# Attention and two feed-forwards on one core: an order that charges for array forms, shared transposes, feed-forward blocks of 512 tokens

## The chip, the cores and the metric

The kernel runs on one core of a Trainium2 chip. The metric is the device time of one execution in microseconds. The kernel before took 1044.32 us, the median of three runs (1043.76 to 1046.07).

## The reference

Three layers follow each other, all in 32-bit floats.

```python
# attention: q, k, v [4, 8, 576, 64], s [4, 8, 576]
scores = q @ k.T / 8                                   # causal
cum = cumsum(maximum(s, 0)); bias = -(cum[i] - cum[j]) # at most 0
attn = softmax(scores + minimum(bias, 0)); x = attn @ v
# heads joined: x [2304, 512]
h = x @ w_in            # [2304, 2048]
x = (h * cos(h)) @ w_out
# x scaled by its root mean square and rms_g, then
y = (silu(xn @ w_gate) * (xn @ w_val)) @ w_out2   # inner width 1536
```

The weights come as float64 and are turned to float32 on the chip.

## The kernel before, in words

**The order.** The program first collects operations (`plan.op`), each with an engine or several that could do it, a cost in ns, the buffers it reads and writes, and a priority, which is a due time (`plan.now`). `Plan.order` then plays them through: the engine that is free first takes, of the operations that are ready, the one with the earliest due time, and its cost moves that engine's clock. The result is a fixed order of instructions on every engine; on the chip each engine works through its own list and waits at semaphores. Two users of one buffer (a slot of a ring, or overlapping bytes of an "arena") are kept in the order in which the program created them.

**Attention.** There are 16 pairs of heads (`Run`, one for each pair). The 576 queries are four tiles of 128 and a ragged one of 64; the ragged rows of the two heads of a pair lie together in one tile of 128 partitions (`"p"`). For each pair TensorE makes the scores: for the full tiles as two products of 64 contraction rows, one for each head, on the two halves of the array (L544; three such operations a pair), for the ragged tile as full products (L568). VectorE adds the bias and takes the minimum (L551, L571), ScalarE takes the exponential (L579), TensorE transposes the probabilities in pieces of 128x128 (`tr`, L594, 30 a pair), ScalarE and VectorE copy them out of PSUM to `Pa` and `Pb`, and TensorE multiplies with v, each head on 64 of the array's columns (L626; two operations a pair). So TensorE works in three forms: the full array, 64 rows by 128 columns (L544), and 128 rows by 64 columns (L626). `tr(e, i)` makes piece group `i` for head `e`. Groups 1 and 3 hold pieces of the ragged tile; both heads transpose the same five 128x128 pieces of it, and each copies its own 64 columns. Scores, transposes and v products of the first four pairs rotate over all eight PSUM banks, those of later pairs over banks 4 to 7 (`Run.bank`, L501). Attention's due times advance by `P_ATT` = 8000 ns a pair.

**First feed-forward.** Tokens go in nine blocks of 256. A step `k` of a block takes two of the 16 slices of 128 inner columns: `gemm1` (L723) makes h for both into one bank, 24 matmuls of 256 columns; ScalarE and VectorE make h * cos(h), split into two parts; `gemm2` (L729) adds 12 matmuls of 512 columns to the block's two accumulators (banks 0 and 1). h rotates over banks 2 and 3, from block 2 on over banks 2, 3 and 4 (`h_bank`). Steps are due every 8094 ns from 45000 ns on. Blocks 0 and 1 run beside attention, and beside block 0 the float64 weights are turned to float32 slices, two chunks of `w_in` and two of `w_out` for each step (`chunk`: L427, L428, L430, then a copy and a subtraction at L333 and L344). `w_out` chunks pass through four slots (`ws_r`), which `gemm2` frees. Blocks 2 to 8 run after attention, whose memory then holds `w_out`. At a block's end `rms_norm` copies its two accumulators out, finds the scale, and `rms_store` transposes (L810) and stores the rows.

**Second feed-forward.** Both products go by a scheme of seven block products in place of eight. `load_x2` loads 768 tokens at a time, forms four sums (`T1` to `T4`) and splits each of seven operands into two parts; `b` counts the three groups of tokens. L973 are the products with `w_gate` and `w_val`, in the order of operands 11, T2, T3, T1, 21, T4, 22; evacuations use slots `t` of 1536 bytes. The 20 slots (`t_spans`) lie in the arena `K`: ten at its upper half, ten at its lower 15 KB, where `load_x2` also stages its sums. L1114 are the products with `w_out2`.

Of the kernel before, what the change touches and what calls it, by code (L numbers as in the profile page):

```python
# [22 lines left out]
BLK1 = 256  # L23
NB1 = NT // BLK1
# [4 lines left out]
RMS_AT = 5  # L29
PAIRED = 0  # L30
# [7 lines left out]
SWITCH_PE = 90.0  # L38
# [11 lines left out]
class Op:  # L50
    __slots__ = ("alts", "prio", "table", "lat", "dma", "preds", "succs", "n", "ready", "eng", "cost", "start", "end", "fn", "seq", "rows")
# [31 lines left out]
class Arena:  # L83


    def __init__(self, plan, make, dtype):
        self.make, self.t, self.dtype, self.bufs = make, None, dtype, []
        plan.arenas.append(self)
# [41 lines left out]
class Plan:  # L130
# [27 lines left out]
    def order(self):  # L158
# [8 lines left out]
        for arena in self.arenas:  # L167
            held = {}
            for b in arena.bufs:
                mine = {o for o, _, _ in b.acc}  # L170
                cells = range(b.at // 256, -(-(b.at + 4 * b.n) // 256))
# [13 lines left out]
        table, dma_free, done, flying = None, 0.0, [], []  # L185
# [34 lines left out]
        while len(done) < len(self.ops):  # L220
# [9 lines left out]
            _, _, o = min((o.prio + (self.HOLD if o.table and o.table != table else 0.0), o.seq, o) for o in avail[e] if o.ready <= t)  # L230
            avail[e].remove(o)
            cost = o.cost
            if e == "PE":
                cost = clock(t, o) - t
# [43 lines left out]
def attention_moe_moe(ctx, tc, q2, k2, vp, s, w_in, w_out, w_gate, w_val, w_out2, rms_g, out):  # L278
# [38 lines left out]
    above = main.tile([128, 128], F32, name="above")  # L317
    pool.memset(above, 0.0)
    pool.affine_select(out=above, in_=above, pattern=[[-1, 128]], base=0, channel_multiplier=1, compare_op=ALU.is_ge, fill=BIG)
# [41 lines left out]
    def later(first, where, size):  # L361
        def make():
            stacks[first].close()
            pools[where] = spool(ctx, where, **ends[where][1])
            return pools[where].tile([128, size * KB // 4], F32R, name=where)
        return make

    A, G, K, R, Z = (Arena(plan, f, t) for f, t in (
        (lambda: wi_t, F32R), (lambda: wg_t, F32R), (lambda: f_t, F32), (later("att", "wr", 64), F32R), (later("x1", "x2", 16), F32R)))
# [12 lines left out]
    y_r = slots(K, 22 * KB, 2, (512,))  # L382
    xo_r = slots(K, 26 * KB, 1, (512,))
    rb_r = slots(K, 28 * KB, 1, (S,))
    st_r = ring("st", 2, [128, 8, 2], F32)
    x1_r = ring("xa", 4, [128, 2, 2, BLK1], F32R, "x1")
# [25 lines left out]
    xn_d = [dbuf(f"xn_d{j}", [128, 4, BLK1]) for j in range(NB1)]  # L412
# [34 lines left out]
    class Run:  # L447
# [52 lines left out]
        def bank(self):  # L500
            return psb("first", (0, 1, 2, 3, 4, 5, 6, 7)) if self.bp < 4 else psb("att", (4, 5, 6, 7))  # L501
# [15 lines left out]
    class Part:  # L517
# [12 lines left out]
        def score(self, ts):  # L530
# [15 lines left out]
            plan.op(on("PE", SWITCH_PE + sum(2.0 * w + 25 for _, w in at.values()), qk), [run.q, run.k], Sp)  # L546
# [11 lines left out]
        def score_p(self, g):  # L558
# [11 lines left out]
            plan.op(on("PE", 490 + SWITCH_PE / 2, qk), [run.q, run.k], [Sp], rows=0.9)  # L570
# [12 lines left out]
        def tr(self, e, i):  # L583
# [3 lines left out]
            srcs = {0: [((e, 0), 0, 128), ((e, 1), 0, 128), ((e, 1), 128, 128)], 1: [((e, 2), 128 * c, 128) for c in range(3)] + [("p", 512, 128)],  # L587
# [8 lines left out]
            plan.op(on("PE", 109 * len(srcs) + 40, go), [(E[0], E[1]) for E in Es], [tr], rows=0.5)  # L596
            cols = lambda n: tr()[:, :n].rearrange("p (c i) -> p c i", i=128)
            def out(o, src, n):
                copy(o, src, n, [tr], [P], psum=True)
# [3 lines left out]
            elif i == 1:  # L603
                out(lambda: P()[:, 0:3, 0:128], lambda: cols(384), 384)
                out(lambda: P()[:, 3, 0:64], lambda: tr()[:, 384 + 64 * e:448 + 64 * e], 64)
            elif i == 2:
                out(lambda: P()[:, :, 128:256], lambda: cols(512), 512)
            else:
                out(lambda: P()[:, :, 256:320], lambda: cols(512)[:, :, 64 * e:64 * e + 64], 256)

        def av(self):
# [16 lines left out]
            plan.op(on("PE", (710 if self.c == "a" else 2130) + SWITCH_PE, go), [vr, *P.values()], [X])  # L628
# [11 lines left out]
        def units(self):  # L640
            if self.c == "a":
# [4 lines left out]
                   [*(lambda e=e, i=i: self.tr(e, i) for i in (1, 3) for e in range(2)), self.av], False, True)  # L646
# [61 lines left out]
    def spin():  # L708
        for _ in range(WARM):
            pe.matmul(warm()[:, :128], ident, above, start=True, stop=True)  # L710
# [25 lines left out]
    def h_bank(j):  # L736
        return psb("h_late", (2, 3, 4)) if j >= RES else psb("h", (2, 3))

    def load_x1(j):
        xs = []  # L740
        for k0 in (0, 2):
            x = x1_r.new()
            raw = lambda x=x: x()[:, :, 1, :].bitcast(F32)
            lo, end = j * BLK1, (j + 1) * BLK1
            while lo < end:
                b, o = lo // S, lo // S * S
                hi = min(end, o + S)
                c0 = lo - j * BLK1
# [3 lines left out]
            copy(lambda x=x: x()[:, :, 0, :], raw, 512, [], [x])  # L752
            two(lambda x=x: x()[:, :, 1, :], raw, lambda x=x: x()[:, :, 0, :].bitcast(F32), 512, [], [x])
# [13 lines left out]
    for j in range(1, NB1):  # L767
        for f in range(F1):
            if j >= RES:
                continue  # L770
# [4 lines left out]
    def rms_norm(j, acc, late=0.0):  # L775
        st, ys = st_r.new(), []
        s0, ms, y, z = ((lambda i=i: st()[:, i, :]) for i in range(4))
        for t in range(2):
            v = y_r.new()
# [22 lines left out]
    def rms_store(j, ys):  # L802
        for k in (0, 2):

            tr, xo = h_bank(j + 1) if j < NB1 - 1 else bank.new(4), ys[0] if k else xo_r.new()

# [9 lines left out]
    acc = {}  # L816
    xs, ticks, todo = {}, {}, []

    def finish(k, h, u, g, less):
        j, m = divmod(k, 8)  # L820
        plan.now = tick_at(k) - LEAD_E
        plan.op(on("ACT", act_s(512) + 93, lambda: act.activation(u(), u(), AF.Sin, scale=-TWO_PI, bias=half_pi)), [], [u], table="sin", after=[less])  # L822
        two(u, h, u, 512, [h], [u], op=ALU.mult, psum=True)
        copy(lambda: g()[:, 0, :], u, 512, [u], [(g, 0)])
        two(lambda: g()[:, 1, :], u, lambda: g()[:, 0, :].bitcast(F32), 512, [u, (g, 0)], [(g, 1)])
        for i in range(2):
            plan.now = tick_at(k) + 1.6 * P_FF1
            f = 2 * m + i
            w = w2[j, f]
            plan.op(on("PE", 1400, lambda i=i, f=f, w=w, a=acc[j]: gemm2(  # L830
                [b() for b in a], [g()[:, a2, BLK1 * i:BLK1 * i + BLK1] for a2 in range(2)], w(), f == 0, f == F1 - 1)), [w, g], acc[j])

    for k in range(8 * NB1):
        j, m = divmod(k, 8)
        plan.now = tick_at(k) - 12000.0
        if m == 0:
            xs[j] = load_x1(j)
            acc[j] = [psb(f"acc{t}", (t,)) for t in range(2)]
        for f in (2 * m, 2 * m + 1):
            if j == RES:  # L840
                w2[j, f] = wr_r.new(f)
                load(lambda f=f: w2[RES, f]().bitcast(F32), wo_d[f], 1 << 19, [wo_d[f]], [w2[j, f]], after=[att_end, ticks[k - 4]])
            elif j > RES:
                w2[j, f] = w2[RES, f]
        h, u, g = h_bank(j), u_r.new(), g_r.new()
        for i in range(2):
            plan.now = tick_at(k)
            w = w1[2 * m + i]
            ticks[k] = plan.op(on("PE", 1440, lambda i=i, w=w, h=h, x=xs[j]: gemm1(h()[:, BLK1 * i:BLK1 * i + BLK1], w(), [b() for b in x], BLK1)), [w, *xs[j]], [h])
        plan.now = tick_at(k) - LEAD_E  # L850
        plan.op(on("ACT", act_p(512) + 93, lambda u=u, h=h: act.activation(u().bitcast(I32), h(), AF.Identity, bias=quarter)), [h], [u])  # L851
        less = two(u, lambda u=u: u().bitcast(I32), h, 512, [h], [u], psum=True)
        todo.append((k, h, u, g))
        if k >= PAIRED or k % 2:
            for args in todo:
                finish(*args, less)
            todo.clear()
        if k % 8 == 1 and j:
            plan.now = tick_at(k) - LEAD_E
            ys = rms_norm(j - 1, acc[j - 1])  # L860
        if k % 8 == RMS_AT and j:
            plan.now = tick_at(k) - LEAD_E
            rms_store(j - 1, ys)
    plan.now = tick_at(8 * NB1)
    rms_store(NB1 - 1, rms_norm(NB1 - 1, acc[NB1 - 1], RMS_LATE))


    T_FF2 = tick_at(8 * NB1 + 1)
# [39 lines left out]
    for n, (d, w, p) in enumerate(jobs):  # L908
        plan.now = tick_at(8 * NB1)
# [5 lines left out]

    X = {}
# [4 lines left out]
    def load_x2(b):  # L921
        for i in range(2):
# [5 lines left out]
            for q, to, o in ((0, raw("11"), x["11"]), (1, B12, B12), (2, raw("21"), x["21"]), (3, raw("22"), x["22"])):  # L928
                k, lo = i + 2 * (q // 2), b * 2 * HALF2 + (q % 2) * HALF2
                end, c0 = lo + HALF2, 0  # L930
                while lo < end:
                    j = lo // BLK1
                    hi = min(end, (j + 1) * BLK1)
                    op = load(lambda to=to, c0=c0, n=hi - lo: to()[:, c0:c0 + n], lambda j=j, k=k, lo=lo, hi=hi: xn_d[j]()[:, k, lo - j * BLK1:hi - j * BLK1],
                              512 * (hi - lo), [(xn_d[j], k // 2 * 2)], [(o, c0)])
                    if q != 1:
# [256 lines left out]
```

## Time and profile before

| | us |
|---|---|
| median of three runs | 1044.32 |
| lowest and highest | 1043.76, 1046.07 |
| the profiled execution | 1041.14 |
| its span, first to last instruction | 1039.40 |
| TensorE matmuls busy in it | 1006.5 |
| VectorE busy | 744.4 |
| ScalarE busy | 574.7 |
| GpSimd busy | 121.1 |
| mean granted clock of TensorE, of full speed | 0.992 |

The profiled execution is one run with the profiler on; its own time stands 1.74 us above its span, and 3.18 us under the median. "Busy" is the time in which at least one instruction of the engine was open. Matmuls overlap, so a busy TensorE still may have instructions of different spacing; the spacing is read from the starts of neighbouring rows.

### The profile page before, as it was taken

How to read it: one execution, taken by the hardware profiler on the slowest of the kernel's cores; microseconds unless marked ns; L12 is line 12 of the kernel's file. 1: busy time of each engine (PE TensorE's matmuls, PEld its weight loads, DVE VectorE, ACT ScalarE, POOL GpSimd, SP SyncE). 2: the span in 40 equal slices, each digit the busy share in tenths (PEclk: the TensorE clock that was granted, in tenths of full speed). 3: DMA queues.
4: the chain of work that ended last, by engine and by line, in shares of the span. 5: the costliest groups of instructions: out<-in, count | busy, mean ns of one | idle time of the engine just before them, and what ended most of it. 6: DMA issues, size and time to landing. Idle time of an engine off the chain costs nothing.

```text
span 1039.4 us, 19161 instructions
## 1 busy us (share of the span) xinstructions
PE 1006.5 (97%) x6594; PEld 897.6 (86%) x6594; DVE 744.4 (72%) x1693; ACT 574.7 (55%) x1236; POOL 121.1 (12%) x251
## 2 busy tenths in 40 slices
PE   7979998999999999999999999899999999999998
PEld 4646666767889999889989989899999999999998
DVE  7885888864436879878877795966566658986661
ACT  5877898897844656666654574311121124665540
POOL 3442453411000011100111000000000000000000
PEclk8999999999999999999999999999999999999999
DMA  8996798775485765657645545466374657997761
GB/s 276 317 334 191 235 309 299 230 247 171 128 296 233 243 239 187 235 196 254 237 169 172 164 125 189 135 204 203 114 233 120 216 177 233 304 318 223 221 196 42
DMA packets 146322, 223.86 MB, mean 215 GB/s; under 512 B 14656, under 2 KB 99792, under 8 KB 146224
## 3 DMA queue, kind: packets, MB, share of 16 engines
q1 hardware_dynamic: 146224, 222.64, 66.3%
q8 instruction: 52, 0.85, 0.3%
q14 instruction: 46, 0.38, 0.1%
HBM read 147.53 MB, written 75.06 MB: 214 GB/s over the span
## 4 chain that ended last, share of the span: by engine, by line
PE 61%; DVE 16%; DMA 12%; issue 5%; ACT 2%; POOL 1%; SPq 1%; POOLq 0%; DVEq 0%; ACTq 0%
PE bank L973 24%; PE bank L1114 13%; PE bank L723 8%; PE bank L729 7%; DVE wk L344 5%; DMA wk<-rn_d 3%; PE bank L626 3%; DVE wg L344 3%; PE bank L594 2%; DVE wk L428 2%; DMA wk<-in_w_out_dram 2%; PE bank L544 2%; DVE wk L430 2%; DMA wk<-in_w_gate_dram 1%; DMA wk<-in_w_val_dram 1%
## 5 line engine op out<-in xcount | busy, mean ns | idle before, releaser
L344 DVE TENSOR_TENSOR wk<-wk,bank 128x384 f32<-128x384 f32 (+2 forms) x315 | 173.0, 555 | 150.9 <-PE bank L973 72.7
L723 PE MATMUL bank<-xa,wi 128*128 128x256 f32 x1728 | 221.3, 283 | 0.1
L723 PEld LDWEIGHTS bank<-xa,wi 128*128 128x128 f32 x1728 | 215.5, 189 | 6.1 <-DVE wi L344 0.3
L729 PE MATMUL bank<-wr,wg 128*128 128x512 f32 x672 | 166.5, 396 | 0.8 <-ACT wg L333 0.7
L729 PEld LDWEIGHTS bank<-wr,wg 128*128 128x128 f32 x672 | 122.3, 188 | 26.8 <-ACT wg L333 1.4
L973 PE MATMUL bank<-wi,wg 128*128 128x384 f32 x504 | 116.8, 340 | 3.8 <-ACT wk L333 2.9
L973 PE MATMUL bank<-wr,wg 128*128 128x384 f32 x504 | 116.9, 340 | 0.0
L344 DVE TENSOR_TENSOR wg<-wk,wg 128x512 fp32r<-128x512 f32 (+1 forms) x148 | 91.4, 636 | 20.0 <-ACT wg L333 19.5
L333 ACT ACTIVATE wk<-bank 128x384 f32<-128x384 f32 (+2 forms) x79 | 40.0, 522 | 116.7 <-PE bank L973 83.6
L333 ACT ACTIVATE wg<-wk 128x512 fp32r<-128x512 f32 (+1 forms) x134 | 75.7, 576 | 49.0 <-DVE wk L344 38.2
L973 PEld LDWEIGHTS bank<-wi,wg 128*128 128x128 f32 x504 | 90.0, 189 | 5.8 <-ACT wk L333 3.4
L344 DVE TENSOR_TENSOR wk<-wk 128x384 f32<-128x384 f32 (+1 forms) x198 | 91.5, 503 | 0.7
L973 PEld LDWEIGHTS bank<-wr,wg 128*128 128x128 f32 x504 | 91.9, 189 | 0.0
L427 POOL TENSOR_SCALAR wk<-wk 128x512 f32<-128x512 f32 x68 | 50.8, 750 | 305.1 <-ACT wk L424 304.2
L579 ACT ACTIVATE e<-e,mn 128x128 f32<-128x128 f32 (+3 forms) x128 | 70.6, 554 | 16.4 <-DVE mn L551 15.8
L344 DVE TENSOR_TENSOR wk<-bank,wk 128x512 f32<-128x512 f32 (+1 forms) x90 | 59.3, 659 | 21.9 <-ACT wk L822 21.7
L822 ACT ACTIVATE wk<-wk,half_pi 128x512 f32<-128x512 f32 x72 | 52.2, 725 | 40.3 <-DVE wk L344 40.0
L333 ACT ACTIVATE wr<-wr 128x384 fp32r<-128x384 f32 x111 | 56.5, 523 | 31.5 <-DMA wr<-g_S 13.0
L1114 PE MATMUL bank<-wi,wr 128*128 128x256 f32 x585 | 73.7, 281 | 0.0
L851 ACT ACTIVATE wk<-bank,quarter 128x512 int32<-128x512 f32 x72 | 49.1, 682 | 41.7 <-PE bank L723 41.5
L1114 PEld LDWEIGHTS bank<-wi,wr 128*128 128x128 f32 x585 | 71.2, 188 | 0.0
L344 DVE TENSOR_TENSOR wr<-wr 128x384 fp32r<-128x384 f32 x111 | 58.0, 552 | 11.7 <-ACT wr L333 11.4
(114 smaller groups left out, 1493.6 us busy)
## 6 DMA issues: line engine op xcount, KB each, us to landing
wk<-in_w_out_dram SPq DMA_DIRECT2D x28, 512.0 KB, 6.5
g_S<-wk SPq DMA_DIRECT2D x72, 192.0 KB, 2.7
g<-wk SPq DMA_DIRECT2D x54, 192.0 KB, 2.4
wr<-g_S SPq DMA_DIRECT2D x54, 192.0 KB, 3.8
w_g<-wg SPq DMA_DIRECT2D x18, 512.0 KB, 4.9
w_v<-wg SPq DMA_DIRECT2D x18, 512.0 KB, 3.4
wr<-g SPq DMA_DIRECT2D x48, 192.0 KB, 3.5
wk<-in_w_in_dram SPq DMA_DIRECT2D x16, 512.0 KB, 5.5
```

The lines of the kernel that those rows point to most:

```text
L333: alts.append(("ACT", (act_p if psum else act_s)(n), lambda: act.activation(o(), i(), AF.Copy, scale=scale)))
L344: return plan.op(on("DVE", dve1(n), lambda: dve.tensor_tensor(out=o(), in0=a(), in1=b(), op=op)), r, w, **kw)
L427: plan.op(on("POOL", pool1(512), lambda: pool.tensor_scalar(out=top().bitcast(F32), in0=top().bitcast(F32), scalar1=0.0, scalar2=1.0, op0= ...
L428: plan.op(on("DVE", dve1(512), lambda: dve.scalar_tensor_tensor(out=top(), in0=low(), scalar=29, in1=top(), op0=ALU.logical_shift_right, o ...
L579: plan.op(on("ACT", act_s(w) + 187, lambda E=E, o=o, w=w, i=i, c=c: act.activation(E()[:, o:o + w], E()[:, o:o + w], AF.Exp, scale=-1.0, b ...
L626: pe.matmul(X()[64 * e:64 * e + 64, lo:hi], vr()[:kk, e, c, :], p[e], start=(c == 0), stop=(c == jobs[-1][0]))
L723: pe.matmul(h, w[:, a, 128 * k:128 * k + 128], x[k // 2][:, k % 2, c, :blk], start=(n == 0), stop=(n == 11))
L729: pe.matmul(acc[t], g[a][:, 128 * t:128 * t + 128], w[:, c, :], start=(first and (a, c) == (0, 0)), stop=(last and (a, c) == (1, 0)))
L822: plan.op(on("ACT", act_s(512) + 93, lambda: act.activation(u(), u(), AF.Sin, scale=-TWO_PI, bias=half_pi)), [], [u], table="sin", after=[ ...
L851: plan.op(on("ACT", act_p(512) + 93, lambda u=u, h=h: act.activation(u().bitcast(I32), h(), AF.Identity, bias=quarter)), [h], [u])
L973: pe.matmul(bank_()[:, :HALF2], G[i]()[:, u, o + 128 * k:o + 128 * k + 128], xs[k]()[:, c, :], start=(first and n == 0), stop=(n == 5), sk ...
L1114: pe.matmul(bk_()[:, col:col + 256], gs[p // 3]()[:, u, 128 * (p % 3):128 * (p % 3) + 128], w3[p][i]()[:, c, o:o + 256], start=(n == 0), s ...
```

## The change

It has these parts.

- **Order.** An operation on TensorE has a `mode` (0 full array, 1 the score products L544, 2 the v products L626). The order charges `SWITCH_PE` = 95 ns where the mode changes, and adds `KEEP_MODE` = 1000 ns to the due time of an operation that would change it. The modelled costs of these operations are changed to fit.
- **Ragged probabilities.** The five pieces of the ragged tile are transposed once for a pair; from the one result both heads' columns are copied.
- **Banks and pace of attention.** The first eight pairs use all eight banks (it was four pairs); `P_ATT` goes from 8000 to 6000.
- **Blocks of the first feed-forward.** Three of 256 tokens (the first two and the last) and three of 512. In a block of 512 a step takes one slice: 12 matmuls of 512 columns in `gemm1`, 12 of 512 columns in `gemm2`, into four accumulators (banks 0, 1, 5, 6). h rotates over banks 2, 3, 4 and 7. `rms_norm` runs twice at such a block's end, the two stores two steps apart.
- **Second feed-forward.** `load_x2` stages operand 11 in the slot of `T4` and makes the operands in the order in which the products take them, both halves of a group together. The `t` slots gain ten in a new arena `Y`, in memory of the x operands of the first feed-forward; these come first in the rotation.
- **Small ones.** The mask tile `above` is gone, and the warm-up multiplies the identity; the x ring holds 512 tokens a slot; the scratch memory for dynamic DMA is set to 1024.

```diff
+KEEP_MODE = 1000.0
-SWITCH_PE = 90.0
+SWITCH_PE = 95.0
-P_ATT, P_FF1, P_SET, P_OUT = 8000.0, 8093.98, 7350.0, 2145.0
+P_ATT, P_FF1, P_SET, P_OUT = 6000.0, 8093.98, 7350.0, 2145.0
+BLOCKS = ((0, 256), (256, 256), (512, 512), (1024, 512), (1536, 512), (2048, 256))
...
-            _, _, o = min((o.prio + (self.HOLD if o.table and o.table != table else 0.0), o.seq, o) for o in avail[e] if o.ready <= t)
+            _, _, o = min((o.prio + (self.HOLD if o.table and o.table != table else 0.0) + (KEEP_MODE if e == "PE" and o.mode != mode else 0.0), o.seq, o)
+                          for o in avail[e] if o.ready <= t)
...
-            return psb("first", (0, 1, 2, 3, 4, 5, 6, 7)) if self.bp < 4 else psb("att", (4, 5, 6, 7))
+            return psb("first", (0, 1, 2, 3, 4, 5, 6, 7)) if self.bp < 8 else psb("att", (4, 5, 6, 7))
...
-                out(lambda: P()[:, :, 256:320], lambda: cols(512)[:, :, 64 * e:64 * e + 64], 256)
+                for a in range(2):
+                    out(lambda a=a: self.P[a]()[:, :, 256:320], lambda a=a: cols(512)[:, :, 64 * a:64 * a + 64], 256, self.P[a])
...
-                   [*(lambda e=e, i=i: self.tr(e, i) for i in (1, 3) for e in range(2)), self.av], False, True)
+                   [*(lambda e=e, i=i: self.tr(e, i) for e, i in ((0, 1), (1, 1), (0, 3))), self.av], False, True)
...
-        return psb("h_late", (2, 3, 4)) if j >= RES else psb("h", (2, 3))
+        return psb("h_late", (2, 3, 4, 7)) if j >= RES else psb("h", (2, 3))
...
+    for j, (lo0, n0) in enumerate(BLOCKS):
+        each, steps = 512 // n0, F1 * n0 // 512
...
+                acc[j] = [psb(f"acc{t}", ((0, 1, 5, 6)[t],)) for t in range(n0 // 128)]
...
+        for name in ("11", "T2", "T3", "T1", "21", "T4", "22"):
+            for i in range(2):
...
-    t_spans = [(K, 15 * KB + i * 1536) for i in range(10)] + [(K, i * 1536) for i in range(10)]
+    t_spans = [(Y, i * 1536) for i in range(10)] + [(K, 15 * KB + i * 1536) for i in range(10)] + [(K, i * 1536) for i in range(10)]
```

## Rows read from the trace of the kernel before

**Rows 1.** The page: busy time of each engine, share of the span, instructions.

```profile
PE 1006.5 (97%) x6594; PEld 897.6 (86%) x6594; DVE 744.4 (72%) x1693; ACT 574.7 (55%) x1236; POOL 121.1 (12%) x251
```

**Rows 2.** Stretches: length, busy us of PE, PEld, DVE, ACT, POOL; granted clock; DMA.

```profile
20.00:93.30 73.30, 64.08 (x434) 39.47 (x433) 57.83 (x174) 58.12 (x174) 32.11 (x76) 0.96 0.95 306
93.30:200.00 106.70, 101.09 (x683) 75.07 (x681) 89.28 (x218) 90.59 (x209) 44.76 (x82) 0.98 0.78 255
200.00:287.70 87.70, 85.46 (x599) 66.46 (x597) 45.79 (x152) 72.18 (x176) 10.46 (x36) 1.00 0.58 183
287.70:622.00 334.30, 333.68 (x2154) 302.03 (x2153) 259.60 (x535) 201.93 (x363) 27.65 (x36) 1.00 0.62 212
...
64.20:67.60 3.40, 2.93 (x16) 1.51 (x16) 2.55 (x5) 0.65 (x3) 1.59 (x4) 0.66 1.03 371
...
658.10:661.50 3.40, 3.40 (x15) 3.40 (x14) 2.78 (x7) 2.59 (x6) 0.00 (x0) 0.65 0.01 2
```

**Rows 3.** The chain that ended last, by time: start, us, what; transposes and feed-forward steps.

```profile
278.14 1.31 PE bank L594 x12
...
297.10 2.85 PE bank L723 x24
299.95 2.73 PE bank L729 x12
...
319.50 2.82 PE bank L723 x24
322.32 2.80 PE bank L729 x12
```

**Rows 4.** TensorE's timeline: four transposes, and the score product that follows.

```profile
105.56 0.49 PE L594 MATMUL bank<-ident,e 128*128 128x128 f32 x3
105.89 0.27 PE L594 MATMUL bank<-ident,ep 128*128 128x128 f32 x1
106.09 1.13 PE L544 MATMUL bank<-kr,qr 64*128 64x512 f32 x4
```

**Rows 5.** TensorE's timeline: the changes of form within one pair.

```profile
245.84 1.13 PE L544 MATMUL bank<-kr,qr 64*128 64x512 f32 x4
...
250.34 0.92 PE L544 MATMUL bank<-kr,qr 64*128 64x384 f32 x4
251.19 2.35 PE L626 MATMUL bank<-Pb,vr 128*64 128x320 f32 x20
...
255.82 0.87 PE L626 MATMUL bank<-Pa,vr 128*64 128x256 f32 x8
...
258.26 0.93 PE L544 MATMUL bank<-kr,qr 64*128 64x128 f32 x8
```

**Rows 6.** TensorE's timeline where it waited longest between 20 and 93 us.

```profile
62.96 1.21 PE L568 MATMUL bank<-kr,qr 128*128 128x288 f32 x2 [2.68 <-DVE mn L551]
```

**Rows 7.** Groups to 287.7 us: VectorE's three operations on a chunk of weights.

```profile
L428 DVE SCALAR_TENSOR_TENSOR wk<-wk 128x512 int32<-128x512 int32 x32 | 22.8, 718 | 7.6 <-POOL wk L427 7.6
L430 DVE SCALAR_TENSOR_TENSOR wk<-wk 128x512 int32<-128x512 int32 x32 | 22.4, 701 | 0.8
L344 DVE TENSOR_TENSOR wi<-wk,wi 128x512 fp32r<-128x512 f32 x16 | 11.0, 688 | 1.0 <-ACT wi L333 0.9
```

**Rows 8.** ScalarE's timeline at a block's end: one accumulator copied out.

```profile
539.23 0.58 ACT L333 ACTIVATE wk<-bank 128x512 f32<-128x512 f32 x1
```

**Rows 9.** TensorE's timeline at the start of the second feed-forward.

```profile
655.55 0.79 PE L973 MATMUL bank<-wi,wg 128*128 128x384 f32 x3 [2.91 <-ACT wk L333]
...
657.28 1.33 PE L973 MATMUL bank<-wi,wg 128*128 128x384 f32 x3 [0.41 <-DVE wk L344]
...
660.92 0.68 PE L973 MATMUL bank<-wi,wg 128*128 128x384 f32 x3
...
663.02 0.68 PE L973 MATMUL bank<-wi,wg 128*128 128x384 f32 x3
```

**Rows 10.** ScalarE's timeline there: the evacuation that released TensorE.

```profile
655.00 0.49 ACT L333 ACTIVATE wk<-bank 128x384 f32<-128x384 f32 x1 [4.46 <-DVE wi L344]
```

More of the change, by code (lines that the diff above doesn't have):

```diff
@@ L43 @@
 BIG = 1.0e9
+BLOCKS = ((0, 256), (256, 256), (512, 512), (1024, 512), (1536, 512), (2048, 256))
 SIZES = {"u": 3, "xr": 1, "xa": 4, "raw": 3}
-P_ATT, P_FF1, P_SET, P_OUT = 8000.0, 8093.98, 7350.0, 2145.0
+P_ATT, P_FF1, P_SET, P_OUT = 6000.0, 8093.98, 7350.0, 2145.0
 T_FF1 = 45000.0
 class Op:
-    __slots__ = ("alts", "prio", "table", "lat", "dma", "preds", "succs", "n", "ready", "eng", "cost", "start", "end", "fn", "seq", "rows")
+    __slots__ = ("alts", "prio", "table", "lat", "dma", "preds", "succs", "n", "ready", "eng", "cost", "start", "end", "fn", "seq", "rows", "mode")
 class Buf:
@@ L233, in order @@
             if e == "PE":
-                cost = clock(t, o) - t
+                cost = clock(t, o) - t + (SWITCH_PE if o.mode != mode else 0.0)
+                mode = o.mode
             if o.table and o.table != table:
@@ L359, in attention_moe_moe, with later @@
     f_t = main.tile([128, 32 * KB // 4], F32, name="wk")
-    def later(first, where, size):
+    def later(first, where, name, size, dtype):
         def make():
-            stacks[first].close()
-            pools[where] = spool(ctx, where, **ends[where][1])
-            return pools[where].tile([128, size * KB // 4], F32R, name=where)
-        return make
-    A, G, K, R, Z = (Arena(plan, f, t) for f, t in (
-        (lambda: wi_t, F32R), (lambda: wg_t, F32R), (lambda: f_t, F32), (later("att", "wr", 64), F32R), (later("x1", "x2", 16), F32R)))
+            if where not in pools:
+                stacks[first].close()
+                pools[where] = spool(ctx, where, **ends[where][1])
+            return pools[where].tile([128, size * KB // 4], dtype, name=name)
+        return make
+    A, G, K, R, Z, Y = (Arena(plan, f, t) for f, t in (
+        (lambda: wi_t, F32R), (lambda: wg_t, F32R), (lambda: f_t, F32), (later("att", "wr", "wr", 64, F32R), F32R),
+        (later("x1", "x2", "x2", 16, F32R), F32R), (later("x1", "x2", "t2", 15, F32), F32)))
     def slots(arena, at, n, shape, dtype=F32):
@@ L411, in attention_moe_moe @@
     x_d = [dbuf(f"x_d{b}", [128, NP, S]) for b in range(B)]
-    xn_d = [dbuf(f"xn_d{j}", [128, 4, BLK1]) for j in range(NB1)]
+    xn_d = [dbuf(f"xn_d{j}", [128, 4, SUB]) for j in range(NT // SUB)]
     wo_d = [dbuf(f"wo_d{f}", [128, 2, 512]) for f in range(F1)]
@@ L544, in qk @@
                         pe.matmul(Sp[e]()[:, o:o + w], run.q()[hd, q0:q0 + 128], run.k()[hd, :w], start=True, stop=True)
-            plan.op(on("PE", SWITCH_PE + sum(2.0 * w + 25 for _, w in at.values()), qk), [run.q, run.k], Sp)
+            plan.op(on("PE", 110 + sum(1.668 * w for _, w in at.values()), qk), [run.q, run.k], Sp, mode=1)
             for t in reversed(ts):
@@ L604, in tr @@
                 out(lambda: P()[:, 0:3, 0:128], lambda: cols(384), 384)
-                out(lambda: P()[:, 3, 0:64], lambda: tr()[:, 384 + 64 * e:448 + 64 * e], 64)
+                for a in range(2) if e == 0 else ():
+                    out(lambda a=a: self.P[a]()[:, 3, 0:64], lambda a=a: tr()[:, 384 + 64 * a:448 + 64 * a], 64, self.P[a])
             elif i == 2:
@@ L709, in spin @@
         for _ in range(WARM):
-            pe.matmul(warm()[:, :128], ident, above, start=True, stop=True)
+            pe.matmul(warm()[:, :128], ident, ident, start=True, stop=True)
     plan.op(on("PE", WARM * 213, spin), [], [warm], prio=-1e6)
@@ L778, in rms_norm @@
         for t in range(2):
-            v = y_r.new()
+            v = (y4_r if late or j > 1 else y_r).new()
             copy(v, acc[t], 512, [acc[t]], [v], psum=True)
@@ L800, in rms_norm, with rms_store @@
         return ys
-    def rms_store(j, ys):
+    def rms_store(j, ys, last=False):
         for k in (0, 2):
-            tr, xo = h_bank(j + 1) if j < NB1 - 1 else bank.new(4), ys[0] if k else xo_r.new()
+            tr, xo = bank.new(4) if last else h_bank(RES if j else 1), ys[0] if k else xo_r.new()
             def go(tr=tr, k=k):
@@ L814, in rms_store @@
             load(lambda k=k: xn_d[j]()[:, k:k + 2, :], lambda xo=xo: xo().rearrange("p (k t) -> p k t", k=2), 1 << 18, [xo], [(xn_d[j], k)], run=2048)
[L816 to L858, printed above, removed]
-            plan.now = tick_at(k) - LEAD_E
[L860 to L863, printed above, removed]
@@ L869, in attention_moe_moe @@
+    k += 1
+    plan.now = tick_at(k)
+    lo0, n0 = BLOCKS[-1]
+    for i in range(n0 // SUB):
+        rms_store(lo0 // SUB + i, rms_norm(lo0 // SUB + i, acc[len(BLOCKS) - 1][2 * i:2 * i + 2], RMS_LATE), True)
+    T_FF2 = tick_at(k + 1)
     OPS = ("11", "12", "22", "S4", "S1", "S2", "S3")
```

128 lines of the change are left out of this document (84 added, 44 removed).

## The prediction

> **What bounds the kernel now.** I read the busy times first. TensorE is busy 1006.5 of 1039.4 us, VectorE 744.4, ScalarE 574.7 [rows 1]; so either TensorE's work shrinks, or its waits do, or nothing moves. The stretches then say where there are waits. From 287.7 to 622 us, the seven later blocks of the first feed-forward, TensorE waits 0.6 us in all. While attention runs it waits 9.2 us between 20 and 93.3 (73.30 less 64.08), 5.6 between 93.3 and 200, and 2.2 between 200 and 287.7; ScalarE and VectorE are busy about 80% in the first of these and about 84% in the second [rows 2]. The reader is to see that attention is nearly but not wholly bound by TensorE, with two other engines close behind, and the first feed-forward wholly.
>
> The other place with a wait is the second feed-forward's start: 2.91 us, then 0.41 [rows 9]. The granted clock falls after it: 0.65 over 658.1 to 661.5, that is mostly the 1.2 GHz level [rows 2]. The price stands in the starts: twelve matmuls of 384 columns from 657.28 to 660.92 take 3.64 us, the next twelve, to 663.02, take 2.10 [rows 9]. So the wait costs 3.3 us and the clock another 1.5. The wait of 2.68 us at 62.96 has the same sequel, a clock of 0.66 from 64.2 to 67.6 [rows 2, 6].
>
> **The change part by part.**
>
> *Ragged transposes.* One piece of group 1 and the four of group 3 go, 5 a pair, 80 in all. Twelve transposes in a row take 1.31 us [rows 3], 109 ns each: 80 x 0.109 = 8.7 us off TensorE. The copies stay as many and as wide, so ScalarE and VectorE gain nothing. Bounds: 8.7 where TensorE is the last to be ready, 0 where another engine is. I take 8.7, since TensorE waits only 17 of the 268 us of this stage. The Trainium skill ("TensorE: Matmul & The Clock Gate", PE-mode transpose) puts such a transpose at about 275 ns inside a kernel; that would make 22 us of this term, but the row, in a dense stream, says 109.
>
> *Changes of form.* Four transposes from 105.56 to the score product at 106.09 take 0.53 us; four at 109 ns would take 0.44. So a change costs about 0.09 us [rows 3, 4]. A pair visits the two small forms five times (245.84, 250.34, 251.19, 255.82, 258.26), and one visit follows another directly: nine changes, some 144 over 16 pairs, 13 us [rows 5]. The penalty of 1000 ns is a sixth of a pair's new pace of 6000, so it can join score products that lie a few operations apart, if their banks are free. With eight banks (the first eight pairs) that is likely now and then; with four, two score operations need all of them. I take two changes a pair for eight pairs and half a change for the rest, 20 x 0.094 = 1.9 us. Bounds: nothing, or four a pair throughout, 6 us.
>
> *Eight banks for pairs 4 to 7, and the pace.* The 2.68 us wait is TensorE held by VectorE's reading of scores (L551) before the next score product has a bank [rows 6]. Pairs 4 to 6, on four banks, run before 93.3 too. Of the 9.2 us idle there I credit 3, about this one wait, and 1 us for the cold stretch that follows it: 4 us. In return the feed-forward's banks 0 to 3 come free only after pair 7, not pair 3, so its first product starts later than 93 us and stands behind attention's due times. That moves work without removing any; I cost it at nothing as long as TensorE has feed-forward steps to fill in with until attention ends. On SP's queue the new pace also puts a pair's loads ahead of weight chunks; DMA is at 0.95 from 20 to 93.3 [rows 2], so chunks land later there, and nothing needs them yet. Bounds: all 17 us of waits and two cold stretches (about 3) gone, 20 us; or a loss, which is the slower case below.
>
> *Blocks of 512.* 48 slices (three blocks of 16) have their h made by 12 matmuls of 512 columns instead of 24 of 256. 24 of 256 take 2.85 and 2.82 us at the first and last of four such steps, 12 of 512 (the second product's) 2.73 and 2.80 [rows 3]: a gain of 0.07 a slice, 3.4 us. TensorE has no cover here, so it counts in full. The number of matmuls of the second product stays. By the Trainium skill ("TensorE: Matmul & The Clock Gate", Back-to-back issue gap) a matmul takes N/2.4 + 2.5 ns: 24 x 109.2 - 12 x 215.8 = 31 ns a slice, an estimate of 1.5 us in all. The rows show both shapes slower than that (118 and 230 ns), the narrow one by more for its work; the term goes by the rows.
>
> *Block edges.* At a 512 edge four accumulators are copied out in place of two, each 0.58 us on ScalarE [rows 8], and two scale computations run back to back on VectorE. Next block's first addition waits for them; TensorE's own h products, 2.8 us a step, lie before it, and a fourth h bank lets it run on. Two engines need some 1.2 us for the copies, so it is covered; if they queue behind other work and the cover is gone, about 2 us and a cold clock's 1.5 at each of three edges. I take 0.5 us lost in all.
>
> *Start of the second feed-forward.* TensorE's 2.91 us wait ends with an evacuation on ScalarE, which itself stood 4.46 us for VectorE's subtraction that splits the last x operands [rows 10]; its `t` slot lies in the bytes where `load_x2` stages. Ten slots elsewhere put the third group's evacuations after that staging, and the new operand order lets the third group begin with operand 11 alone. I take 4 of the 4.8 us. What is late next is VectorE, which splits 14 operands at 0.5 us each beside the evacuations. Bounds: 4.8 gained, or 1 lost.
>
> *The small parts.* `above` held the warm-up only, which ends before the first q and k arrive: nothing. The x loads and splits of a 512 block are twice as wide and half as many, with the same bytes: nothing.
>
> The sum: 8.7 + 1.9 + 4 + 3.4 - 0.5 + 4 = 21.5 us. The profiled execution took 1041.14, so 1019.6 for one like it; the median of the runs stands 3.18 higher at 1044.32, and for the median I forecast 1023 us.
>
> **The rivals.**
>
> *More than forecast* (about 1008). All waits of attention go, and score products join: 16 us more in the third term, capped by ScalarE. For it: the waits behind four banks. Against: ScalarE and VectorE at 84% [rows 2].
>
> *Attention bound by ScalarE and VectorE* (about 1037). Then the transposes, form changes and banks give nothing, and 7.4 - 0.5 stays. For it: those 80 to 85%. Against it: TensorE waits 2.2 us in 87.7 at the stage's end, with ScalarE at 72.18.
>
> *Block edges stall* (about 1033): three times 3.5 us, as above. Against it: VectorE is at 259.60 of 334.30 there, and TensorE never waits [rows 2].
>
> *Slower: feed-forward steps left alone with the weights.* Attention is now due at 6000 ns a pair and a step at 8094, so when the last pair is due (91 us) only (91 - 45)/8.1, between five and six, steps are. If attention takes TensorE first, steps of block 0 are left for after it. Such a step needs four chunks, on VectorE 4 x (718 + 701 + 688) = 8.4 us [rows 7] and some 2 us for its own three operations, 10.4 against 5.6 on TensorE: 4.8 us lost for each step left alone. From 4.5 steps on (21.5/4.8) the change is a loss; with all eight it is 1061. For it: chunks stop at four of `w_out` until the feed-forward starts, which is later now. Against: before, TensorE filled all 16 steps in by 287.7.
>
> **How the numbers follow.** Chances: forecast 0.57 (its own range 1014 to 1030), more 0.16, ScalarE and VectorE 0.13, edges 0.05, slower 0.09. The range 1008 to 1040 leaves out the slower case and half of the first rival. A change of 0.2% (2.1 us) is what runs of this kernel can tell from none. Faster than that: 0.57 + 0.16 + 0.05 and most of the third, 0.86; within it 0.05; slower 0.09.
>
> **What would show it.** 400 transposes (480 before) still 109 ns apart; 576 matmuls of 256 and 576 of 512 columns in the first product, 12 of the latter in under 2.8 us; TensorE's wait before its third group of tokens under 1 us, at full clock; attention and the first two blocks over near 272 us; no waits at the block edges. Wrong it is if that stage ends after 285, or if TensorE's idle time there grows past 30 us.

## The result and the profile after

The changed kernel takes 1013.57 us (median of four runs, 1010.95 to 1017.0), the kernel before 1044.04 us beside it: a ratio of 0.9713, 95% interval 0.9673 to 0.9753. That is 30 us less where 21 were forecast. It lies inside the stated range of 1008 to 1040, 9 us below the point, and 0.4 us below the forecast's own 1014 to 1030, on the side of the rival "more than forecast". Ratios compare the means of undisturbed executions; one execution of the nine-block kernel (2643.02 us) and the one profiled of "Before, with the shared transposes alone" (1086.77 us, at a mean granted clock of 0.847) are left out of them. The profiled execution took 1012.63 us against 1041.14, so the traces have 28.5 us to explain.

The page of the changed kernel, busy times by engine, beside [rows 1]. TensorE has 656 matmul records fewer; VectorE, ScalarE and GpSimd do the same work as before within 2%.

```profile
span 1010.7 us, 17819 instructions
PE 992.4 (98%) x5938; PEld 857.9 (85%) x5938; DVE 748.1 (74%) x1701; ACT 564.3 (56%) x1215; POOL 122.3 (12%) x246
```

I cut both traces where block 2 of the first feed-forward makes its first product (302.5 and 282.6 us), where the last first product of that layer ends, and where the second feed-forward's first part ends. First the kernel before, stretches with the columns of [rows 2] (new rows, since these cuts are not those shown earlier):

```profile
20.00:302.50 282.50, 265.43 (x1803) 194.25 (x1803) 198.62 (x551) 227.18 (x567) 87.33 (x194) 0.98 0.77 247
302.50:622.10 319.60, 318.98 (x2062) 288.87 (x2061) 253.97 (x528) 195.65 (x353) 27.65 (x36) 1.00 0.61 210
622.20:901.00 278.80, 274.81 (x1546) 271.46 (x1546) 191.68 (x387) 79.86 (x167) 0.00 (x0) 0.99 0.62 190
```

And the same three of the changed kernel:

```profile
20.00:282.60 262.60, 253.93 (x1721) 183.12 (x1722) 202.76 (x564) 218.48 (x554) 87.75 (x191) 0.99 0.84 272
282.60:600.40 317.80, 317.70 (x1486) 260.94 (x1485) 252.38 (x520) 193.65 (x346) 29.04 (x36) 1.00 0.59 205
600.40:872.40 272.00, 272.00 (x1547) 270.36 (x1546) 192.04 (x390) 79.60 (x166) 0.00 (x0) 1.00 0.64 193
```

The reader is to see three gains. Attention and blocks 0 and 1 end 19.9 us earlier; TensorE's idle time there falls from 17.1 (282.50 less 265.43) to 8.7 us, and 82 matmul records go, 80 of them the transposes. The later blocks gain 1.8 us. The second feed-forward's first part gains 6.8 us: TensorE waited 4.0 us in it, now never, and the clock stays up.

The cut at 302.5 also shows that a mark of the prediction was misread. At 287.7 us the kernel before ends attention, but only 14 of the 16 steps of blocks 0 and 1 have made their h; the other two follow up to 302.5. So "attention and the first two blocks over near 272" mixes two marks. After the change attention ends at 252 us, and the h of the two blocks is made by 282.6, where 302.5 less the 14.6 us of the three attention terms gives 288.

The forms of the changed kernel's matmuls (count, busy us, mean ns) answer the forecast's counts: 400 transposes in two groups, and the first product in halves.

```profile
L598 PE MATMUL bank<-ident,e 128*128 128x128 f32 x320 | 50.0, 282 | 5.4 <-ACT e L583 2.9 <-DVE Pb L337 1.2 <-DVE mn L555 0.7
L598 PE MATMUL bank<-ident,ep 128*128 128x128 f32 x80 | 14.5, 286 | 0.8 <-ACT ep L583 0.5 <-ACT Pb L334 0.2
L729 PE MATMUL bank<-xa,wi 128*128 128x512 f32 x576 | 142.0, 396 | 0.0
L729 PE MATMUL bank<-xa,wi 128*128 128x256 f32 x576 | 75.5, 284 | 0.6 <-ACT Pb L334 0.6
```

The chain of the changed kernel, across the edge from block 1 (256 tokens) to block 2 (512), beside [rows 3]:

```profile
277.21 2.85 PE bank L729 x24
280.06 2.73 PE bank L735 x12
282.79 2.81 PE bank L729 x12
285.60 2.73 PE bank L735 x12
288.33 2.81 PE bank L729 x12
```

A slice's h takes 2.81 us in twelve wide matmuls and 2.85 in 24 narrow ones: 0.04 less, not 0.07. The prediction's sign "under 2.8 us" was missed by a hundredth; the transposes do stand 109 ns apart (the median in a run of them).

### The profile page after: what moved, and what is told of

Its sections match the earlier page's. It is cut to its first block, busy times and chain, and to the rows that moved or that the text cites. A ratio compares the mean times of both kernels' runs of the same rounds, so it can differ in the third digit from the quotient of the medians.

```text
span 1010.7 us, 17819 instructions
## 1 busy us (share of the span) xinstructions
PE 992.4 (98%) x5938; PEld 857.9 (85%) x5938; DVE 748.1 (74%) x1701; ACT 564.3 (56%) x1215; POOL 122.3 (12%) x246
## 4 chain that ended last, share of the span: by engine, by line
PE 70%; DVE 10%; DMA 6%; issue 5%; ACT 2%; POOL 1%; SPq 1%; POOLq 0%; DVEq 0%; ACTq 0%
PE bank L985 26%; PE bank L1126 13%; PE bank L729 12%; PE bank L735 11%; DVE wk L345 3%; DVE wg L345 2%; PE bank L632 2%; PE bank L598 2%; DMA wk<-in_w_gate_dram 2%; PE bank L548 2%; DVE wk L432 1%; DVE wk L434 1%; DMA wk<-rn_d 1%; DMA wk<-in_w_val_dram 1%; PE bank L572 1%
## 5 line engine op out<-in xcount | busy, mean ns | idle before, releaser
L729 PE MATMUL bank<-xa,wi 128*128 128x256 f32 (+1 forms) x1152 | 217.5, 340 | 0.6 <-ACT Pb L334 0.6
L345 DVE TENSOR_TENSOR wk<-wk,bank 128x384 f32<-128x384 f32 (+2 forms) x237 | 130.4, 555 | 117.7 <-ACT wk L845 43.7
L729 PEld LDWEIGHTS bank<-xa,wi 128*128 128x128 f32 x1152 | 179.5, 188 | 32.4 <-issue 4.0
L735 PEld LDWEIGHTS bank<-wr,wg 128*128 128x128 f32 x672 | 125.2, 188 | 29.6 <-ACT wg L334 0.9
L334 ACT ACTIVATE wg<-wk 128x512 fp32r<-128x512 f32 (+1 forms) x132 | 74.7, 580 | 51.9 <-DVE wk L345 34.6
L985 PEld LDWEIGHTS bank<-wr,wg 128*128 128x128 f32 x504 | 91.3, 188 | 0.0
L334 ACT ACTIVATE wr<-wr 128x384 fp32r<-128x384 f32 x108 | 55.4, 524 | 40.5 <-DMA wr<-g_S 21.8
L583 ACT ACTIVATE e<-e,mn 128x512 f32<-128x512 f32 (+3 forms) x128 | 70.6, 555 | 12.9 <-DVE mn L555 12.3
L334 ACT ACTIVATE wk<-bank 128x512 f32<-128x512 f32 (+2 forms) x66 | 33.9, 532 | 70.3 <-PE bank L985 53.8
L345 DVE TENSOR_TENSOR wk<-bank,wk 128x512 f32<-128x512 f32 (+1 forms) x82 | 54.7, 667 | 20.8 <-ACT wk L847 20.6
L345 DVE TENSOR_TENSOR t<-t,bank 128x384 f32<-128x384 f32 x72 | 39.6, 551 | 30.0 <-PE bank L985 28.2
```

Source lines behind the costliest of these rows:

```text
L334: alts.append(("ACT", (act_p if psum else act_s)(n), lambda: act.activation(o(), i(), AF.Copy, scale=scale)))
L345: return plan.op(on("DVE", dve1(n), lambda: dve.tensor_tensor(out=o(), in0=a(), in1=b(), op=op)), r, w, **kw)
L583: plan.op(on("ACT", act_s(w) + 187, lambda E=E, o=o, w=w, i=i, c=c: act.activation(E()[:, o:o + w], E()[:, o:o + w], AF.Exp, scale=-1.0, b ...
L729: pe.matmul(h, w[:, a, 128 * k:128 * k + 128], x[k // 2][:, k % 2, c, :blk], start=(n == 0), stop=(n == 11))
L735: pe.matmul(acc[t], g[a][:, 128 * t:128 * t + 128], w[:, c, :], start=(first and (a, c) == (0, 0)), stop=(last and (a, c) == (1, 0)))
L985: pe.matmul(bank_()[:, :HALF2], G[i]()[:, u, o + 128 * k:o + 128 * k + 128], xs[k]()[:, c, :], start=(first and n == 0), stop=(n == 5), sk ...
```

## The experiments

Each was timed beside the kernel before: the first four on one chip, the next four and the last four on two others (medians of the kernel before 1042.89, 1041.81 and 1042.47). A ratio's interval reaches about 0.003 (3 us) to either side, more than the 0.2% that the prediction took, and a difference of two ratios is uncertain by some 4 us. So a difference of 1 to 3 us is not read from the times. Times "more" are differences of ratios to the changed kernel's 0.972 of the first experiment, times 1043 us. Stretches run from 20 us to the first product of block 2, as above; length less TensorE's busy time is its wait.

**The changed kernel again.** No edit.

> The changed kernel once more, as the mark that the other runs of this chip are held against. 1012 to 1016 us, 0.971 of the kernel before.

1014.0 us, ratio 0.9720 [0.9689, 0.9751]. This is the mark. Its trace is a second one of the same kernel, and shows how far two executions of it stand apart in the first stretch:

```profile
20.00:283.90 263.90, 253.71 (x1719) 181.60 (x1718) 203.93 (x564) 218.36 (x552) 86.91 (x191) 0.99 0.84 271
```

It is 1.3 us longer than the first trace's 262.60. TensorE waits 10.2 us in place of 8.7, and is busy 0.2 us less. By these two, a difference of under 2 us in the length or the waits of this stretch shows nothing, while busy time repeats.

**Ragged tile transposed for each head.**

```diff
-[("p", 512, 128)] * (e == 0)
+[("p", 512, 128)]
-for e, i in ((0, 1), (1, 1), (0, 3))
+for i in (1, 3) for e in range(2)
```

> The changed kernel, but the ragged tile is transposed for each head again (480 transposes, not 400). If TensorE's own work bounds the attention stage: 80 x 109 ns = 8.7 us more than the changed kernel, about 1022. Rival (ScalarE and VectorE bound it): at most 2 us more, and TensorE's waits before 260 us are shorter by about as much as the transposes add.

1024.1 us (1022.13 to 1026.83), ratio 0.9818 [0.9786, 0.9851]: 10.2 us more. Its stretch:

```profile
20.00:293.50 273.50, 260.78 (x1803) 189.69 (x1802) 202.27 (x560) 219.67 (x555) 89.45 (x193) 1.00 0.81 261
```

10.9 us longer than the changed kernel's 262.60: TensorE is busy 6.9 us more and waits 12.7 in place of 8.7 us (10.2 in the second trace), and the clock's share is 1.00, not 0.99. The transposes stand on the path; the rival (other engines bound it) falls.

**Nine blocks of 256.**

```diff
-BLOCKS = ((0, 256), (256, 256), (512, 512), (1024, 512), (1536, 512), (2048, 256))
+BLOCKS = tuple((256 * j, 256) for j in range(9))
```

> The changed kernel with nine blocks of 256 tokens. By the prediction's term 3.4 us more, about 1017. Rival, from the changed kernel's trace, where 12 matmuls of 512 columns in the first product stand 234 ns apart (2.81 us) beside 24 of 256 at 118 (2.83): 1 us more or less, 1013 to 1015.

1016.02 us, ratio 0.9728 [0.9696, 0.9761]: 0.8 us more, inside the noise. The stretch of the later blocks:

```profile
284.30:603.20 318.90, 318.67 (x2061) 288.37 (x2060) 252.83 (x524) 194.35 (x350) 28.75 (x36) 1.00 0.58 203
```

318.9 against 317.8 us, 1.1 more, of which 1.0 is busy time. The wide blocks are worth about 1 us; the term of 3.4 was too large.

**Eight banks for four pairs alone.**

```diff
-if self.bp < 8 else psb("att", (4, 5, 6, 7))
+if self.bp < 4 else psb("att", (4, 5, 6, 7))
```

> The changed kernel, but pairs 4 to 7 on banks 4 to 7 alone, as before. Theory (the bank rule removed the waits before 93 us and let attention end early): 4 to 9 us more, 1018 to 1022, with the wait of the score products for VectorE's L555 back at pairs 4 to 7. Rival (the pace of 6000 did it): under 2 us more.

1020.57 us (1018.17 to 1022.96), ratio 0.9781 [0.9750, 0.9811]: 6.4 us more. Its stretch, and its longest wait of a ragged score product for VectorE (us in total, times, longest):

```profile
20.00:288.20 268.20, 255.42 (x1722) 182.31 (x1721) 202.24 (x570) 218.90 (x546) 92.35 (x192) 0.99 0.80 267
```
```profile
PE bank L572 <- DVE mn L555: 2.3, 1, 2.3
```

The waits grow by 4.1 us to 12.8. The rest, 1.5 us, is busy time. Counted over all rows of TensorE's timeline the form changes 136 times, against 126 in the changed kernel and 145 before, and ten changes at 0.094 us would be 0.9 of it. The long wait for L555 is back, but at 189 us, where both kernels give attention four banks; between 55 and 92 us there are eight waits of 0.2 to 1.2 us. So the size was right and the place was not.

**Attention due every 8000 ns.**

```diff
-P_ATT, P_FF1, P_SET, P_OUT = 6000.0, 8093.98, 7350.0, 2145.0
+P_ATT, P_FF1, P_SET, P_OUT = 8000.0, 8093.98, 7350.0, 2145.0
```

> The changed kernel with attention due every 8000 ns a pair, as before. Theory of the banks: under 2 us more than the changed kernel (1013.6). Rival (the pace did it): 4 to 9 us more, and attention ends later than at 252 us by as much.

1016.25 us, ratio 0.9742 [0.9713, 0.9771]: 2.3 us more, not clear of the noise.

```profile
20.00:284.70 264.70, 251.23 (x1719) 181.50 (x1718) 199.96 (x564) 224.96 (x561) 81.81 (x184) 1.00 0.81 264
```

The stretch is 2.1 us longer than the changed kernel's first trace, and 0.8 than its second: 13.5 us of waits in place of 8.7 or 10.2, and 2.7 or 2.5 us less busy, with a clock of 1.00 in place of 0.99. Attention ends 12 us later than in the changed kernel (the last v product starts at 263.5 us, not 251.9), and blocks 0 and 1 end nearly as early: the pace decides mostly what TensorE does first. That it is worth anything in time is not shown.

**No penalty on a change of form.**

```diff
-KEEP_MODE = 1000.0
+KEEP_MODE = 0.0
```

> The changed kernel without the 1000 ns on operations that change the array's form; the 95 ns charge stays. The changed kernel's order has 126 changes of form against 145 before: if these are the penalty's doing, 19 x 0.094 = 1.8 us more. Rival: the order comes out worse or better elsewhere by more than that, 3 us or more either way.

1016.61 us, ratio 0.9744 [0.9716, 0.9772]: 2.5 us more. The form changes 138 times, twelve more than in the changed kernel. Twelve changes at 0.094 us are 1.1 us. The stretch is 1.6 us longer than the first trace's, and 0.3 than the second's:

```profile
20.00:284.20 264.20, 254.58 (x1721) 181.25 (x1722) 200.50 (x565) 216.94 (x547) 92.92 (x195) 0.99 0.85 271
```

Busy time is up by 0.7 us on the first trace and 0.9 on the second, near the 1.1 of the theory; the length is inside the scatter. A further 1.4 us lie in the later blocks (319.2 us from block 2's first product, not 317.8), as waits for ScalarE. So the times do not tell the penalty from nothing, and the trace shows its changes of form and hardly more.

**No slots in the arena Y.**

```diff
-    t_spans = [(Y, i * 1536) for i in range(10)] + [(K, 15 * KB + i * 1536) for i in range(10)] + ...
+    t_spans = [(K, 15 * KB + i * 1536) for i in range(10)] + ...
-    t_last = Slots(t_spans[:20], (HALF2,), F32)
+    t_last = Slots(t_spans[:10] + t_spans[-2:], (HALF2,), F32)
```

> The changed kernel with the 20 evacuation slots of before, without the ten in the arena Y. Theory (the slots held the third group's first evacuation behind the staging of the operands): the wait of 3 us and its cold stretch come back, 4 to 6 us more. Rival (the order of the operands did it): under 1 us more.

1018.76 us, ratio 0.9771 [0.9742, 0.9800]: 5.3 us more. TensorE's timeline at the third group of tokens, then the clock there:

```profile
637.33 1.31 PE L985 MATMUL bank<-wi,wg 128*128 128x384 f32 x3 [3.52 <-ACT wk L334]
638.45 1.16 PE L985 MATMUL bank<-wr,wg 128*128 128x384 f32 x3
```
```profile
637.40:640.80 3.40, 3.40 (x11) 3.40 (x12) 3.40 (x9) 2.02 (x5) 0.00 (x0) 0.50 0.16 47
```

The wait of [rows 9] is back, released as in [rows 10] by an evacuation on ScalarE that stands behind VectorE's splitting of the operands, and the half clock follows it.

**Operands in the old order.**

```diff
-        for name in ("11", "T2", "T3", "T1", "21", "T4", "22"):
-            for i in range(2):
+        for i in range(2):
+            for name in ("11", "T4", "21", "22", "T1", "T2", "T3"):   # T1, T2, T3 summed first
```

> The changed kernel with the operands of the second feed-forward made in the old order, one half of the group after the other. Theory of the slots: under 1 us more. Rival (the operand order did it): 3 to 6 us more, with a wait before the third group's first product.

1019.76 us, ratio 0.9768 [0.9739, 0.9798]: 5.0 us more. (The order within a half is nearly the old one: T4 stands second, since operand 11 is staged in its slot.) The same place on TensorE:

```profile
640.50 1.01 PE L981 MATMUL bank<-wr,wg 128*128 128x384 f32 x2 [2.30 <-DVE wr L345]
641.31 1.16 PE L981 MATMUL bank<-wi,wg 128*128 128x384 f32 x3
642.27 1.16 PE L981 MATMUL bank<-wr,wg 128*128 128x384 f32 x3
644.24 0.79 PE L981 MATMUL bank<-wi,wg 128*128 128x384 f32 x3 [0.81 <-DVE wk L345]
```

TensorE now has the first half's operand 11 and stands for the second half's, which VectorE reaches after all seven of the first half. Both theories were half right: either edit taken away brings back a wait of 3 us. They remove two waits that cover each other. The whole gain there was 6.8 us, and taking either away costs 5, so either one alone in the kernel before should be worth some 2 us; that was not run.

**Before, with the shared transposes alone.** The edit is the reverse of the second experiment, in the kernel before.

> The kernel before with one edit, the ragged tile transposed once for a pair. If TensorE's work bounds attention there too: 8.7 us less, about 1034. Rival (before, the waits on four banks took up what TensorE is spared): under 3 us less, with TensorE's waits between 20 us and the end of block 1 longer than 17 us by the rest.

1028.52 us, ratio 0.9854 [0.9822, 0.9886]: 15.2 us less than before (11.9 to 18.6). The whole interval lies above 8.7, so more went than the transposes' own time. Whether that was waits or clock, and where, is not shown; no trace of this kernel is used.

**Before, with eight banks for eight pairs alone.**

```diff
-if self.bp < 4 else psb("att", (4, 5, 6, 7))
+if self.bp < 8 else psb("att", (4, 5, 6, 7))
```

> The kernel before with one edit, all eight banks for pairs 0 to 7. Theory of the banks: 5 to 8 us less, waits from 20 us to the end of block 1 near 10 us, the first feed-forward's start later than 93 us, near 107. Rival (the rule helps only beside the pace of 6000): within 2 us of before.

1029.29 us, ratio 0.9869 [0.9838, 0.9900]: 13.7 us less.

```profile
20.00:292.30 272.30, 263.76 (x1802) 190.50 (x1802) 193.06 (x548) 227.14 (x572) 82.38 (x188) 1.00 0.81 259
```

That is more than the 5 to 8 expected; the first feed-forward starts at 105.6 us, as expected. With the same transposes, the same pace and the same 145 changes of form the waits fall from 17.1 to 8.5 us, and the clock is at 1.00, not 0.98: a stretch like that of 64.2 to 67.6 [rows 2] is not seen here. The stretch is 10.2 us shorter. Up to the feed-forward's start the waits fall from 9.2 to 4.2 us, and after it from 7.8 to 4.4. That is the bank rule by itself, and what the prediction put at 4 us. The rival (only with the pace of 6000) falls.

**Eight banks for six pairs.**

```diff
-if self.bp < 8 else psb("att", (4, 5, 6, 7))
+if self.bp < 6 else psb("att", (4, 5, 6, 7))
```

> The changed kernel with eight banks for six pairs, not eight. If each pair on eight banks before the feed-forward starts spares a wait, half of what four pairs cost (6.5 us): 3 us more than the changed kernel. Rival (the start of the feed-forward at 93 us is worth as much): 0 to 2 us less.

1021.66 us, ratio 0.9790 [0.9753, 0.9826]: 7.3 us more, as bad as four pairs; both expectations missed. Its stretch, its longest wait on TensorE, and ScalarE's timeline before it:

```profile
20.00:292.30 272.30, 256.95 (x1720) 183.76 (x1719) 202.83 (x569) 217.78 (x547) 90.73 (x192) 0.97 0.81 263
```
```profile
91.86 1.65 PE L548 MATMUL bank<-kr,qr 64*128 64x384 f32 x2 [4.83 <-ACT xu L334]
```
```profile
89.04 0.66 ACT L428 ACTIVATE wk<-wk 128x512 f32<-128x512 f32 x1 [2.22 <-DMA wk<-in_w_in_dram]
91.37 0.71 ACT L334 ACTIVATE xu<-bank 128x320 f32<-128x320 f32 x2 [1.67 <-DMA x_d<-xu]
```

TensorE waits for a bank, the bank for its copy on ScalarE, and ScalarE's list stands first for a chunk of weights still in flight and then for an earlier result's store. From within the wait on, 88.2 to 98.4 us, the clock is at 0.50. DMA is busy there (0.93 from 20 to 105 us), and a copy that ScalarE's list has behind a transfer comes late. Full DMA is not enough by itself: in the tenth experiment its share is 0.99 from 20 to 105.6 us, and no wait of TensorE in that stretch passes 1.6 us. I had seen the banks and not this.

**Eight banks for ten pairs.**

```diff
-if self.bp < 8 else psb("att", (4, 5, 6, 7))
+if self.bp < 10 else psb("att", (4, 5, 6, 7))
```

> The changed kernel with eight banks for ten pairs. The first feed-forward then starts near 128 us, and weights stop at four chunks of w_out until then. By the prediction's slower case, steps of block 0 are left alone with the weights: 3 to 15 us more, with waits of TensorE for VectorE after attention's end. Rival (banks are worth more than an early start): 0 to 3 us less.

1025.36 us, ratio 0.9830 [0.9798, 0.9862]: 11.5 us more. Stretches up to the start of the feed-forward, then to 200, to attention's end, and to block 2:

```profile
20.00:128.60 108.60, 100.36 (x681) 62.18 (x679) 80.60 (x270) 91.72 (x284) 42.23 (x111) 0.94 0.94 292
128.60:200.00 71.40, 65.02 (x421) 47.34 (x419) 56.59 (x134) 60.32 (x129) 22.78 (x45) 1.00 0.70 228
200.00:255.30 55.30, 51.35 (x358) 36.45 (x360) 47.04 (x122) 49.79 (x116) 17.75 (x32) 1.00 0.79 252
255.30:295.80 40.50, 40.50 (x267) 36.75 (x264) 18.02 (x36) 16.93 (x30) 0.00 (x0) 1.00 0.72 235
```

The size is in the expected range, but not by the path that was named: the waits lie beside attention (8.2 us up to the start, 6.4 to 200, 4.0 to 255.3), and none after it. The slower case is there in small: 4.2 of the 6.4 us are feed-forward products waiting for VectorE or ScalarE, 1.5 of them for chunks of `w_in`. None of these kernels is faster than the changed one.

## Why the prediction was right, and where a size was off

**The bound.** Right. TensorE is not busy for 18.3 us of the span (1010.7 less 992.4), against 32.9 before, and the time went where its work or its waits went.

**Ragged transposes, 8.7 us.** Right in place, and the size holds within the experiment: 10.2 us when undone, with busy time 6.9 of it. The 22 us that the prediction set beside it is another quantity: one transpose is open for 282 to 286 ns (the rows of the changed kernel), but its neighbours start 109 ns apart, and the 80 put back in the second experiment cost 6.9 us of busy time, 86 ns each. In the kernel before the term was worth more, 15.2; what went along there is not shown.

**Changes of form, 20 fewer, 1.9 us.** 19 fewer (145 to 126). The penalty accounts for 12, as the sixth experiment counts, and the banks are its condition, as the prediction said: with eight banks for four, six, eight and ten pairs the form changes 136, 131, 126 and 119 times. The price holds too: in the changed kernel the first score or v product starts 0.203 us after the last transpose (the median of 33), against 0.109 from transpose to transpose. So 19 changes are 1.8 us. No run's time shows it by itself, and the charge of 95 ns and the altered costs were not tried alone.

**Banks and pace, 4 us.** The mechanism was right, the size was the term most off. In the kernel before the bank rule alone shortens the stretch by 10.2 us, 8.5 of it waits; from the changed kernel it is worth 6.4. The term credited 3 of the 9.2 us up to 93, about the one wait of 2.68 us [rows 6], and 1 us of clock, and left the 7.8 us after 93 as they were; they went to 1.8. The changed kernel's stretches up to the feed-forward's start, to 200 and to 267 us wait 6.8, 1.8 and 0.1:

```profile
20.00:106.40 86.40, 79.56 (x536) 50.05 (x536) 70.07 (x224) 74.28 (x229) 36.16 (x94) 0.96 0.98 309
106.40:200.00 93.60, 91.82 (x628) 66.91 (x629) 82.71 (x213) 84.09 (x198) 41.20 (x76) 1.00 0.84 278
200.00:267.00 67.00, 66.95 (x461) 51.98 (x460) 44.92 (x121) 54.60 (x120) 10.39 (x21) 1.00 0.64 206
```

Why the later waits go as well is not settled. That the feed-forward now has more of its steps left to fill in with is an argument; the ten-pair kernel, which leaves still more and waits more, speaks against it as the whole reason. The pace by itself moved 2 us, inside the noise. The two terms overlap: alone in the kernel before, the transposes and the banks are worth 15.2 and 13.7 us, together 28.9, and taken from the changed kernel one at a time 10.2 and 6.4, together 16.6; attention as a whole gained 19.9. Adding up terms that were each priced alone cannot be exact here.

**Blocks of 512, 3.4 us.** Too large: 1.1 us. The step that failed took the second product's spacing for the first product's. Twelve wide matmuls of the first product take 2.81 us where twelve of the second take 2.73 to 2.80. The Trainium skill ("TensorE: Matmul & The Clock Gate", Back-to-back issue gap) gives its gap for a matmul by itself; the prediction's estimate from it was 1.5 us for this term. That lies nearer to the 1.1 than the 3.4 does, though in this stream both shapes run slower than that gap: 234 and 119 ns here, 216 and 109 there.

**Block edges, 0.5 us lost.** TensorE waits 0.1 us from 282.6 to 600.4. The four copies are covered.

**Start of the second feed-forward, 4 us.** The mechanism was right, and it takes both edits, as experiments seven and eight show. The size was 6.8 us for the stretch: 4.0 of waits and 1.5 of clock account for 5.5 (the waits include 0.5 us at 879 that I had not counted), and the other 1.3 us, all busy time, is not accounted for.

**The rivals.** ScalarE and VectorE as the bound: against it speak the second and ninth experiments. Edges: no. More than forecast: in part, since half of attention's waits went, though no more changes of form than forecast. Slower: attention ended at 252 us with five steps of block 1 left and none of block 0 alone with the weights. Its argument against, that the kernel before had filled in all 16 steps by 287.7, was wrong (14 had made their h); even so the case did not come about, and at pair 10 its cost came beside attention.

The sum over the traces: 19.9 + 1.8 + 6.8 = 28.5 us, all that lies between the two executions; the forecast for them was 21.5. Attention came out 5.3 us above its terms (14.6), the second feed-forward 2.8 above, the later blocks 1.1 below (2.9 with the edges). That the last took something off the other two is luck.

## What to carry to other kernels

In this case work taken off the bounding engine was priced well from rows of that same instruction, and badly from a neighbour's. Waits removed were out by a factor of 1.7 to 2.6 (6.8 and 10.2 us where 4 was forecast each time); that the next order of the instructions brings or spares other waits is the likely reason. A second trace of the same kernel tells what a difference between traces is worth. Where two conditions hold the same instruction, such as a buffer and an operand, test each alone: here taking out either edit brought a wait of 3 us back. And a rule of the order, such as how many pairs get eight banks, need not be best near its best value on one side: four, six, eight and ten pairs gave 6.4, 7.3, 0 and 11.5 us more.

## What the runs showed that I had not expected

A wait of 2.5 us in attention is followed by a stretch at the lower clock: the changed kernel's v product at 92.84 takes 3.67 us for the 20 matmuls that take 2.27 at 78.78, at a granted clock of 0.50, the 1.2 GHz level.

```profile
78.78 2.27 PE L632 MATMUL bank<-Pb,vr 128*64 128x320 f32 x20
90.78 0.28 PE L513 MATMUL bank<-ident,rs 128*9 128x128 f32 x1 [2.47 <-ACT xu L334]
92.84 3.67 PE L632 MATMUL bank<-Pb,vr 128*64 128x320 f32 x20
```
```profile
90.29 0.71 ACT L334 ACTIVATE xu<-bank 128x320 f32<-128x320 f32 x2 [1.06 <-DMA x_d<-xu]
```
```profile
92.30:95.70 3.40, 3.40 (x14) 1.38 (x14) 3.16 (x10) 2.00 (x6) 0.59 (x2) 0.50 1.10 237
```

That wait too is in part one of ScalarE's list standing for a store (L334, `xu`, 1.06 us), the chain of the six-pair kernel. It is the longest wait of TensorE after 20 us, and no run tried to remove it.
